# Output tiles in shared space, weight preparation four steps in, and paired column groups in an expert layer on one core

## The chip, the cores and the metric

One NeuronCore of a Trainium2 chip runs the whole program in one launch. The metric is the device time in microseconds (us); the program before took 934.85 us, the median of three runs (929.9 to 939.41).

## What is computed

Three stages follow each other. Stage one is a linear attention: `phi` projects queries and keys, takes exponentials, and num/den gives a token matrix x of 2304 x 512 floats. Stage two is a mixture of eight experts: each token goes to the expert with the largest gate logit, and

```
h = np.maximum(x[mask] @ w1[e], 0.0)            # 512 -> 1024
out[mask] = gate_w[mask, None] * (h @ w2[e])    # 1024 -> 512
```

Stage three is a gated network over all tokens:

```
a = x @ w_a;  b = x @ w_b                       # 512 -> 1536 each
return (a * b @ w_out).astype(np.float32)       # 1536 -> 512
```

The weights of stage three arrive as 64-bit floats; everything else is 32-bit, and the result is 32-bit. To keep 32-bit accuracy each operand of a matmul is split into a high and a low part (`mm3`, L51 to L54: three matmuls per product).

## The kernel before, in words

The kernel is written in a tile framework that places the semaphores and, for each engine, fixes one order of instructions at compile time by a planner: it walks the program in its own simulated time and gives a free engine the ready instruction with the smallest priority number. The number is the place in the program; `high_priority(offset=-LOWP)` adds 200 to it, so that such work yields to work written up to 200 instructions later. On the chip each engine then works through its fixed order, and an instruction that waits holds up all behind it. PE's order in stage three is written out by hand (`manual_schedule`).

**Stage two** (`Moe`, L518 on). The tokens of either half (two halves, `routes[0]` and `routes[1]`) are sorted by expert into tiles of 608 places, two groups of 304 columns each; here there are four tiles (called tile 0 to tile 3), with eight steps each, 32 steps in all (`run`, L603). In a tile's steps 0 to 3 `l1` runs for two f each (f = 0 to 7): for each column group 12 matmuls into a PSUM tile of one bank (`ps_l`, six buffers), then ScalarE writes `hh` (the rectified high part, L588) and VectorE `hl` (the rest, L589). In steps 4 to 7 `l2` runs: for each column group 24 matmuls over f = 0 to 7 (L600), then ScalarE copies the result (L601). Beside them: `loadw` and `splitw` bring the expert's weights (L542, L550, L551), and `gather` and `transp` bring the next tile's tokens in five pieces (L559, L571; their high and low parts `mxh` L574 and `mxl` L575); the transposes use the two buffers of `ps_t`, which the routing of the second half (`Route`, started from `side` at steps 0, 2, 4 and 6, L947) shares for its tables (`tbp`, `tbq`, L495).

**Weight preparation** (`Moe2.prep`, L699, with `narrow`, L677). The stage-three weights are cut into 12 pieces of f. `prep` turns one piece from 64 to 32 bits in two halves: a load `raw` of 768 KB (SyncE, L684), ScalarE (L688), GpSimd (L689), five VectorE instructions (L690 to L697); then sums (L706 to L709), the split into high and low (L714, L715), and four stores to `wsc` in DRAM (L716, L717). `raw` has two buffers in its pool. Eight pieces (NPRE) are prepared beside stage two, written at the steps `K0 + (K1 - K0) * f // 8`, which are steps 0, 3, 6, 10, 13, 16, 20 and 23 (L955 to L957). At step K1 = 27 `open_first` (L964) gives back their space and loads the first weights of stage three. The other four are prepared in stages 0, 2, 4 and 6 of stage three, from a second pool, `cv2` (L979 to L982).

**Between the two** stands a conditional (`tc.If`, L975) for more tiles than four; it is not entered here.

**Stage three** (`Moe2.run`, L779). There are 36 stages: three pairs of column blocks p, times 12 pieces f. A stage computes seven products `abp` (L830 to L834) in two PSUM buffers (`ps_l2`); ScalarE copies each out (`pc`, L836), VectorE combines them, and `outp` (L802) adds to six accumulators `op` (one bank each, one buffer each) for the stage before. After the last f of a p, `finish` (L784) scales the six accumulators into `o`, alternately on ScalarE (L793) and VectorE (L791), and GpSimd stores each by an indirect DMA (L794). `o` has OB = 2 buffers.

Of the kernel before, what the change touches and what calls it, by code (L numbers as in the profile page):

```python
# [10 lines left out]
F32 = mybir.dt.float32  # L11
F32R = mybir.dt.float32r
BF16 = mybir.dt.bfloat16
I32 = mybir.dt.int32
AF = mybir.ActivationFunctionType
ALU = mybir.AluOpType
AX = mybir.AxisListType
PSUM = bass.MemoryType.PSUM
ds = bass.ds

P = 128
# [3 lines left out]
DM = H * D  # L25
# [5 lines left out]
CG = 304  # L31
# [5 lines left out]
TB = 6  # L37
NPRE = 8
LOWP = 200
OB = 2  # L40
LOWP2 = 60
NWARM = 9
NATIVE = (0,)
# [3 lines left out]
def f32(ap):  # L47
    return ap.bitcast(F32)


def mm3(nc, out, lh, ll, rh, rl, start, stop):  # L51
    nc.tensor.matmul(out, lh, rh, start=start, stop=False)  # L52
    nc.tensor.matmul(out, lh, rl, start=False, stop=False)  # L53
    nc.tensor.matmul(out, ll, rh, start=False, stop=stop)  # L54
# [463 lines left out]
class Moe:  # L518
# [58 lines left out]
    def l1(self, T, f):  # L577
        nc = self.nc
        wh, wl = T["w", f // 2]
        for g in range(2):  # L580
            gs = slice(g * CG, g * CG + CG)
            ps = self.ps_l.tile([P, 512], F32, tag="l", name="hp")
            for c in range(4):
                i = 4 * (f % 2) + c
                mm3(nc, ps[:, :CG], wh[:, i, :], wl[:, i, :], T["xh"][:, c, gs], T["xl"][:, c, gs], c == 0, c == 3)
            hh = self.p_h.tile([P, CG], F32R, tag=f"h{f}{g}", name="hh")
            hl = self.p_h.tile([P, CG], F32R, tag=f"l{f}{g}", name="hl")
            nc.scalar.activation(hh, ps[:, :CG], AF.Relu)  # L588
            nc.vector.scalar_tensor_tensor(out=hl, in0=ps[:, :CG], scalar=0.0, in1=f32(hh), op0=ALU.max,  # L589
                                           op1=ALU.subtract)  # L590
            T["h", f, g] = (hh, hl)

    def l2(self, T, m):
        nc = self.nc
        wh, wl = T["w", 4 + m]
        for g in range(2):
            ps = self.ps_l.tile([P, 512], F32, tag="l", name="yp")
            for f in range(8):
                hh, hl = T["h", f, g]
                mm3(nc, ps[:, :CG], wh[:, f, :], wl[:, f, :], hh, hl, f == 0, f == 7)  # L600
            nc.scalar.copy(self.y[T["rt"].bp][:, m, ds(T["s"][g], CG)], ps[:, :CG])  # L601

    def run(self, tiles, side={}):  # L603
        NT, NJ = len(tiles), self.NJ
# [48 lines left out]
class Moe2:  # L653
# [13 lines left out]
    def pools(self, ctx, ps_a, ps_l):  # L667
        tc = self.tc
        pool = lambda n, b: ctx.enter_context(tc.tile_pool(name=n, bufs=b, side="right", reuse_waits="tile"))
        self.p_w[1] = pool("f_w1", 1)  # L670
        self.p_t[1] = pool("f_t1", 4)
        self.p_c = pool("f_c", 1)
        self.p_g = pool("f_g", 2)
        self.p_o = pool("f_o", OB)
        self.ps_a, self.ps_l = ps_a, ps_l

    def narrow(self, pool, f, half, dst, nt):  # L677
# [101 lines left out]
    def run(self, ws, ts, src0, side):  # L779
        nc, n = self.nc, self.N  # L780
        seq = [(p, f) for p in range(NTOK // n // 2) for f in range(self.NF)]
        accs, gs = {}, {}

        def finish(p):  # L784
            for m, acc in enumerate(accs.pop(p)):
                bp, b = divmod(2 * p + m // 3, HALF // n)
                o = self.p_o.tile([P, DM], F32, tag="o", name="o")
                c = b * (n // P) + m % 3
                g2 = self.routes[bp].g2[:, c:c + 1]
                if m % 2:  # L790
                    nc.vector.tensor_scalar(out=o, in0=acc, scalar1=g2, scalar2=None, op0=ALU.mult)  # L791
                else:
                    nc.scalar.activation(o, acc, AF.Copy, scale=g2)  # L793
                st = nc.gpsimd.indirect_dma_start(  # L794
                    out=self.out[:, :],
                    out_offset=bass.IndirectOffsetOnAxis(ap=self.routes[bp].perm[:, c:c + 1], axis=0),
                    in_=o[:, :], in_offset=None)
                for other in self.stores:
                    self.tc.declare_no_dep(st.ins, other, reason="each row of the output is stored once")
                self.stores.append(st.ins)  # L800

        def outp(k, m):  # L802
            p, f = seq[k]
            if f == 0 and m == 0:
                accs[p] = [self.ps_a.tile([P, 512], F32, tag=f"a{i}", name=f"op{i}") for i in range(6)]
            gh, gl = gs[k]
            wh, wl = ws[k](1536, 512)
            ms = slice(P * (m % 3), P * (m % 3) + P)
            mm3(nc, accs[p][m], gh[:, m // 3, ms], gl[:, m // 3, ms], wh, wl, f == 0, f == self.NF - 1)
            if m == 5:  # L810
                del gs[k], ws[k]
                if f == self.NF - 1:
                    finish(p)

        def stage(k):
            p, f = seq[k]
            ct = lambda tag, shape: self.p_c.tile([P] + shape, F32, tag=tag, name=tag)
            ca, u, d = ct("ca", [2, n]), ct("u", [2, n]), ct("d", [2, n])
            out = []
            gs[k] = [self.p_g.tile([P, 2, n], F32R, tag=t, name=t) for t in ("gh", "gl")]  # L820

            def gate(i, other):
                gh, gl = (x[:, i, :] for x in gs[k])
                nc.vector.tensor_mul(ca[:, i, :], ca[:, i, :], other)
                nc.scalar.copy(gh, ca[:, i, :])  # L825
                nc.vector.tensor_sub(gl, ca[:, i, :], f32(gh))  # L826

            for i, (col, t) in enumerate(self.PROD):
                ps = self.ps_l.tile([P, 512], F32, tag="l", name="abp")[:, :n]
                wh, wl = ws[k](col, 256)  # L830
                th, tl = ts[p][t]
                for c in range(2):
                    cs = slice(P * c, P * c + P)
                    mm3(nc, ps, wh[:, cs], wl[:, cs], th[:, c, :], tl[:, c, :], c == 0, c == 1)  # L834
                x = self.p_c.tile([P, n], F32, tag="pc", name="pc", bufs=5)
                nc.scalar.copy(x, ps)  # L836
                out.append(x)
                if i == 1:
                    nc.vector.tensor_add(u[:, 0, :], x, out[0])
                elif i == 2:  # L840
                    nc.vector.tensor_add(ca[:, 0, :], x, out[0])
                elif i == 3:
                    nc.vector.tensor_add(u[:, 1, :], x, u[:, 0, :])  # L843
                elif i == 4:
                    nc.vector.tensor_add(d, u, x.unsqueeze(1).to_broadcast([P, 2, n]))
                elif i == 5:
                    nc.vector.tensor_add(x, x, u[:, 1, :])
                    gate(0, x)
                elif i == 6:
                    nc.vector.tensor_add(ca[:, 1, :], x, d[:, 0, :])  # L850
                    gate(1, d[:, 1, :])
                if k and i > 1:
                    for m in (i - 2,) if i < 6 else (4, 5):
                        outp(k - 1, m)

        src = src0
        self.rest(src, ts[0])
        for k, (p, f) in enumerate(seq):
            with self.tc.high_priority(offset=-LOWP2):
                for st in side.get(k, ()):  # L860
                    st()
            if k + 1 < len(seq) and k + 1 not in ws:
                ws[k + 1] = self.weights(k + 1)
            if f == 0 and p:
                self.rest(src, ts[p])
            with self.tc.manual_schedule(engines={mybir.EngineType.PE}):
                stage(k)
            if f == self.NF - 2 and k + 2 < len(seq):
                src, ts[p + 1] = self.terms(p + 1, self.p_s)
        with self.tc.manual_schedule(engines={mybir.EngineType.PE}):  # L870
            for m in range(6):
                outp(len(seq) - 1, m)
# [13 lines left out]
def trn_kernel(ctx, tc, qk, v, w_phi, mod_id, w_gate, bias, wm, wf, out):  # L886
    nc = tc.nc
# [8 lines left out]
    tl = dict(reuse_waits="tile")  # L896
# [24 lines left out]
                       {5: rsteps[0:2], 6: rsteps[2:3], 7: rsteps[3:4]}.get(r, []) if r > 2 else [])  # L921
    with ExitStack() as mctx:
        ps_t = mctx.enter_context(tc.tile_pool(name="ps_t", bufs=2, space=PSUM, **tl))
        ps_l = mctx.enter_context(tc.tile_pool(name="ps_l", bufs=6, space=PSUM, **tl))
        ypool = ctx.enter_context(tc.tile_pool(name="y", bufs=1, **tl))
        y = [ypool.tile([P, 4, YC], F32, name=f"y{i}") for i in range(2)]
        m2 = Moe2(nc, tc, wf, wsc, y, routes, out, f64)
        mo = Moe(nc, tc, mctx, cst, xs, wm, y, ps_l, ps_t)
# [23 lines left out]
            with tc.high_priority(offset=-LOWP):  # L952
                m2.prep(f, cv[0], 2, 2)

        K0, K1 = 0, len(tiles) * mo.NJ - 5  # L955
        for f in range(NPRE):
            side.setdefault(K0 + (K1 - K0) * f // NPRE, []).append(lambda f=f: conv(f))  # L957
        ts, src0 = {}, []
# [24 lines left out]
    ps_a = ctx.enter_context(tc.tile_pool(name="ps_a2", bufs=1, space=PSUM, **tl))  # L983
    ps_l = ctx.enter_context(tc.tile_pool(name="ps_l2", bufs=2, space=PSUM, **tl))
    m2.pools(ctx, ps_a, ps_l)
    m2.run(ws, ts, src0[0], side)


# [55 lines left out]
```

## Time and profile before

| what | value |
|---|---|
| median of three runs | 934.85 us (929.9 to 939.41) |
| the profiled execution's own time | 940.45 us |
| its span, first to last instruction | 938.7 us |
| PE busy | 880.0 us (94%), granted clock 0.957 on the mean |
| VectorE (DVE) busy | 671.3 us (72%) |
| ScalarE (ACT) busy | 438.3 us (47%) |
| GpSimd (POOL) busy | 187.4 us (20%) |

The engines' busy time is a mean over the three stages. PE here is the matmul engine, PEld its weight loads, SP the SyncE queue that issues most DMAs. [...] Stage one ends at about 246 us, stage two at about 481 us, stage three's last matmul at 926.4 us.

### The profile page before, as it was taken

What the parts mean: (1) busy time and instruction counts of PE and PEld (TensorE: products, weight loads), DVE (VectorE), ACT (ScalarE), POOL (GpSimd) and SP (SyncE); (2) the same over time, 40 slices, a digit from 0 to 9 for tenths busy, and PEclk for the clock granted to TensorE, in tenths of its full rate; (3) what the DMA queues carried; (4) which work ended last, traced back from release to release, by engine and by line L of the source; (5) the groups of instructions that cost most, each with busy time, mean ns of one, the idle gap of its engine ahead of it and who ended that gap; (6) DMA issues with size and microseconds to landing.
All of it is one profiled execution on the core that took longest, in us unless ns stands there. A gap on an engine that the chain in (4) does not pass through costs nothing. (4 is left out here: it accounts for less than half of the span.)

```text
span 938.7 us, 15310 instructions
## 1 busy us (share of the span) xinstructions
PE 880.0 (94%) x5645; PEld 833.4 (89%) x5645; DVE 671.3 (72%) x1252; ACT 438.3 (47%) x806; POOL 187.4 (20%) x171
## 2 busy tenths in 40 slices
PE   6899999899799799999989999978999998999994
PEld 4899998899799799999988989967999998999993
DVE  7878899969799998986239889856454466554552
ACT  5577666555344454554324445444333344333332
POOL 6443333301343543220002111002000001000002
PEclk7999998899899799999989999979999999999998
DMA  7332330112567688795037998586666667766631
GB/s 246 102 104 77 105 105 13 29 57 64 199 203 268 245 287 307 277 322 188 29 131 290 371 317 312 189 305 206 213 202 205 203 201 244 223 203 202 202 124 67
DMA packets 74309, 179.21 MB, mean 191 GB/s; under 512 B 8912, under 2 KB 27808, under 8 KB 74224
## 3 DMA queue, kind: packets, MB, share of 16 engines
q1 hardware_dynamic: 71184, 168.39, 53.3%
q0 software_dynamic: 3040, 9.75, 3.1%
q8 instruction: 46, 0.75, 0.3%
q14 instruction: 39, 0.32, 0.1%
HBM read 140.36 MB, written 37.75 MB: 190 GB/s over the span
## 5 line engine op out<-in xcount | busy, mean ns | idle before, releaser
L836 ACT COPY pc<-abp 128x384 f32<-128x384 f32 x252 | 120.4, 479 | 195.6 <-PE abp L54 193.9
L52 PE MATMUL abp<-yh,fw 128*128 128x384 f32 x504 | 173.6, 344 | 16.1 <-DMA fw<-wsc 6.4
L54 PE MATMUL abp<-yh,fw 128*128 128x384 f32 x504 | 172.6, 342 | 0.2 <-DMA fw<-wsc 0.2
L53 PE MATMUL abp<-yl,fw 128*128 128x384 f32 x504 | 172.4, 342 | 0.0
L52 PEld LDWEIGHTS abp<-yh,fw 128*128 128x128 f32 x504 | 97.0, 192 | 25.9 <-ACT pc L836 7.6
L689 POOL TENSOR_SCALAR cvs<-cvs 128x768 f32<-128x768 f32 x24 | 59.2, 2468 | 250.4 <-ACT cvs L688 244.9
L53 PEld LDWEIGHTS abp<-yl,fw 128*128 128x128 f32 x504 | 97.0, 192 | 7.8
L54 PEld LDWEIGHTS abp<-yh,fw 128*128 128x128 f32 x504 | 96.7, 192 | 0.7 <-DMA fw<-wsc 0.7
L54 PE MATMUL op<-fw,gl 128*128 128x512 f32 x216 | 85.9, 398 | 1.3 <-DVE gl L826 1.3
L52 PE MATMUL op<-fw,gh 128*128 128x512 f32 x216 | 86.1, 398 | 1.0 <-ACT gh L825 1.0
L53 PE MATMUL op<-fw,gh 128*128 128x512 f32 x216 | 85.4, 395 | 0.0
L794 POOL DMA_INDIRECT out<-o,perm x18 | 17.7, 983 | 318.5 <-ACT o L793 311.7
L53 PE MATMUL hp<-mxl,wh 128*128 128x304 f32 x256 | 79.1, 310 | 1.5 <-DVE mxl L575 1.5
L52 PE MATMUL hp<-mxh,wh 128*128 128x304 f32 x256 | 79.5, 314 | 0.6 <-ACT mxh L574 0.6
L54 PE MATMUL hp<-mxh,wl 128*128 128x304 f32 x256 | 78.7, 308 | 0.0
L53 PE MATMUL yp<-hl,wh 128*128 128x304 f32 x256 | 77.3, 303 | 0.0
L52 PE MATMUL yp<-hh,wh 128*128 128x304 f32 x256 | 77.0, 303 | 0.0
L54 PE MATMUL yp<-hh,wl 128*128 128x304 f32 x256 | 77.0, 302 | 0.0
L236 PE MATMUL nmp<-kx,qts 128*128 128x73 f32 (+1 forms) x640 | 73.3, 271 | 1.8 <-DVE grest L478 1.8
L236 PEld LDWEIGHTS nmp<-kx,qts 128*128 128x128 f32 (+1 forms) x640 | 69.7, 187 | 4.0 <-issue 3.0
L185 ACT ACTIVATE qts<-qtp 128x512 f32<-128x512 f32 (+1 forms) x80 | 40.2, 552 | 47.0 <-PE qtp L182 46.8
L127 POOL TENSOR_TENSOR xtl<-qk,xth 128x512 fp32r<-128x512 f32 (+1 forms) x35 | 44.3, 1268 | 88.0 <-ACT xth L126 83.0
(201 smaller groups left out, 2052.9 us busy)
## 6 DMA issues: line engine op xcount, KB each, us to landing
fw<-wsc SPq DMA_DIRECT2D x72, 512.0 KB
fw<-wsc SPq DMA_DIRECT2D x144, 256.0 KB
raw<-in_moe_w SPq DMA_DIRECT2D x24, 768.0 KB
s<-in_moe_w SPq DMA_DIRECT2D x32, 512.0 KB
fw<-wsc SPq DMA_DIRECT2D x72, 128.0 KB
wsc<-whi SPq DMA_DIRECT2D x12, 640.0 KB
wsc<-wsum SPq DMA_DIRECT2D x12, 640.0 KB
wsc<-whi SPq DMA_DIRECT2D x12, 512.0 KB
```

The lines of the kernel that those rows point to most:

```text
L52: nc.tensor.matmul(out, lh, rh, start=start, stop=False)
L53: nc.tensor.matmul(out, lh, rl, start=False, stop=False)
L54: nc.tensor.matmul(out, ll, rh, start=False, stop=stop)
L127: (nc.vector if u == 0 else nc.gpsimd).tensor_sub(lo[:, x:y], src, f32(hi[:, x:y]))
L185: nc.scalar.activation(t[:, s, :n, :], ps[:, :n, :], AF.Exp, scale=1.0 - 2.0 * s)
L236: nc.tensor.matmul(ps[pp, o, :], qt[:, c, a, pp], st["kx", b][:, 2 * h + c, :], start=c == 0, stop=c == 1)
L689: nc.gpsimd.tensor_scalar(out=s.bitcast(F32), in0=s.bitcast(F32), scalar1=LEAST, scalar2=None, op0=ALU.max)
L794: st = nc.gpsimd.indirect_dma_start(out=self.out[:, :], out_offset=bass.IndirectOffsetOnAxis(ap=self.routes[bp].perm[:, c:c + 1], axis=0), ...
L836: nc.scalar.copy(x, ps)
```

## The change

Three edits stand in one diff.

In `finish` three accumulators now share one tile `os` of 3 x 512 floats, with tag `raw` in the pool `cv2`: it has the size of a `raw` tile (6144 bytes per partition) and takes its two buffers, so that six outputs have room at once. The pool `f_o` and OB are gone. The scaling and the stores are as before, each on a third of a tile.

K0 and K1 are 3 and 28: the eight preparations are written at steps 3, 6, 9, 12, 15, 18, 21 and 24, and `open_first` at step 28.

In `l1` one PSUM tile of two banks holds both column groups; after the 24 matmuls of an f there is one ScalarE and one VectorE instruction over 2 x 304 columns where there were two of each over 304. `hh` and `hl` are one tile per f. `l2` also takes a tile of two banks, a bank per group, and copies each bank as before. `ps_l` has three such tiles where it had six of one bank.

```diff
--- before.py
+++ after.py
@@ -37,7 +37,6 @@
 TB = 6
 NPRE = 8
 LOWP = 200
-OB = 2
 LOWP2 = 60
 NWARM = 9
 NATIVE = (0,)
@@ -577,28 +576,28 @@
     def l1(self, T, f):
         nc = self.nc
         wh, wl = T["w", f // 2]
+        ps = self.ps_l.tile([P, 2, 512], F32, tag="l", name="hp")
         for g in range(2):
             gs = slice(g * CG, g * CG + CG)
-            ps = self.ps_l.tile([P, 512], F32, tag="l", name="hp")
             for c in range(4):
                 i = 4 * (f % 2) + c
-                mm3(nc, ps[:, :CG], wh[:, i, :], wl[:, i, :], T["xh"][:, c, gs], T["xl"][:, c, gs], c == 0, c == 3)
-            hh = self.p_h.tile([P, CG], F32R, tag=f"h{f}{g}", name="hh")
-            hl = self.p_h.tile([P, CG], F32R, tag=f"l{f}{g}", name="hl")
-            nc.scalar.activation(hh, ps[:, :CG], AF.Relu)
-            nc.vector.scalar_tensor_tensor(out=hl, in0=ps[:, :CG], scalar=0.0, in1=f32(hh), op0=ALU.max,
-                                           op1=ALU.subtract)
-            T["h", f, g] = (hh, hl)
+                mm3(nc, ps[:, g, :CG], wh[:, i, :], wl[:, i, :], T["xh"][:, c, gs], T["xl"][:, c, gs], c == 0, c == 3)
+        hh = self.p_h.tile([P, 2, CG], F32R, tag=f"h{f}", name="hh")
+        hl = self.p_h.tile([P, 2, CG], F32R, tag=f"l{f}", name="hl")
+        nc.scalar.activation(hh, ps[:, :, :CG], AF.Relu)
+        nc.vector.scalar_tensor_tensor(out=hl, in0=ps[:, :, :CG], scalar=0.0, in1=f32(hh), op0=ALU.max,
+                                       op1=ALU.subtract)
+        T["h", f] = (hh, hl)
 
     def l2(self, T, m):
         nc = self.nc
         wh, wl = T["w", 4 + m]
+        ps = self.ps_l.tile([P, 2, 512], F32, tag="l", name="yp")
         for g in range(2):
-            ps = self.ps_l.tile([P, 512], F32, tag="l", name="yp")
             for f in range(8):
-                hh, hl = T["h", f, g]
-                mm3(nc, ps[:, :CG], wh[:, f, :], wl[:, f, :], hh, hl, f == 0, f == 7)
-            nc.scalar.copy(self.y[T["rt"].bp][:, m, ds(T["s"][g], CG)], ps[:, :CG])
+                hh, hl = T["h", f]
+                mm3(nc, ps[:, g, :CG], wh[:, f, :], wl[:, f, :], hh[:, g, :], hl[:, g, :], f == 0, f == 7)
+            nc.scalar.copy(self.y[T["rt"].bp][:, m, ds(T["s"][g], CG)], ps[:, g, :CG])
 
     def run(self, tiles, side={}):
         NT, NJ = len(tiles), self.NJ
@@ -671,7 +670,6 @@
         self.p_t[1] = pool("f_t1", 4)
         self.p_c = pool("f_c", 1)
         self.p_g = pool("f_g", 2)
-        self.p_o = pool("f_o", OB)
         self.ps_a, self.ps_l = ps_a, ps_l
 
     def narrow(self, pool, f, half, dst, nt):
@@ -784,7 +782,9 @@
         def finish(p):
             for m, acc in enumerate(accs.pop(p)):
                 bp, b = divmod(2 * p + m // 3, HALF // n)
-                o = self.p_o.tile([P, DM], F32, tag="o", name="o")
+                if m % 3 == 0:
+                    os = self.p_o.tile([P, 3, DM], F32, tag="raw", name="o", bufs=2)
+                o = os[:, m % 3, :]
                 c = b * (n // P) + m % 3
                 g2 = self.routes[bp].g2[:, c:c + 1]
                 if m % 2:
@@ -794,7 +794,7 @@
                 st = nc.gpsimd.indirect_dma_start(
                     out=self.out[:, :],
                     out_offset=bass.IndirectOffsetOnAxis(ap=self.routes[bp].perm[:, c:c + 1], axis=0),
-                    in_=o[:, :], in_offset=None)
+                    in_=o, in_offset=None)
                 for other in self.stores:
                     self.tc.declare_no_dep(st.ins, other, reason="each row of the output is stored once")
                 self.stores.append(st.ins)
@@ -921,7 +921,7 @@
                        {5: rsteps[0:2], 6: rsteps[2:3], 7: rsteps[3:4]}.get(r, []) if r > 2 else [])
     with ExitStack() as mctx:
         ps_t = mctx.enter_context(tc.tile_pool(name="ps_t", bufs=2, space=PSUM, **tl))
-        ps_l = mctx.enter_context(tc.tile_pool(name="ps_l", bufs=6, space=PSUM, **tl))
+        ps_l = mctx.enter_context(tc.tile_pool(name="ps_l", bufs=3, space=PSUM, **tl))
         ypool = ctx.enter_context(tc.tile_pool(name="y", bufs=1, **tl))
         y = [ypool.tile([P, 4, YC], F32, name=f"y{i}") for i in range(2)]
         m2 = Moe2(nc, tc, wf, wsc, y, routes, out, f64)
@@ -952,7 +952,7 @@
             with tc.high_priority(offset=-LOWP):
                 m2.prep(f, cv[0], 2, 2)
 
-        K0, K1 = 0, len(tiles) * mo.NJ - 5
+        K0, K1 = 3, len(tiles) * mo.NJ - 4
         for f in range(NPRE):
             side.setdefault(K0 + (K1 - K0) * f // NPRE, []).append(lambda f=f: conv(f))
         ts, src0 = {}, []
@@ -983,6 +983,7 @@
     ps_a = ctx.enter_context(tc.tile_pool(name="ps_a2", bufs=1, space=PSUM, **tl))
     ps_l = ctx.enter_context(tc.tile_pool(name="ps_l2", bufs=2, space=PSUM, **tl))
     m2.pools(ctx, ps_a, ps_l)
+    m2.p_o = cv[1]
     m2.run(ws, ts, src0[0], side)
```

## Rows read from the trace of the kernel before

**Rows 1.** Waits of PE, whole span: releaser, total us, times, longest us.
```profile
PE abp L52 <- DMA fw<-wsc: 6.4, 1, 6.4
PE abp L52 <- ACT pc L836: 6.1, 4, 2.9
...
PE abp L54 <- DMA fw<-wsc: 0.2, 1, 0.2
```

**Rows 2.** By stretch: us; PE, PEld, DVE, ACT, POOL busy (count); PEclk; DMA; GB/s.
```profile
246.00:313.50 67.50, 61.58 (x447) 60.63 (x445) 63.29 (x142) 31.38 (x51) 29.75 (x13) 0.93 0.61 205
...
373.60:427.30 53.70, 53.70 (x390) 53.69 (x391) 48.64 (x70) 27.28 (x45) 13.46 (x6) 1.00 0.85 302
427.30:484.70 57.40, 53.74 (x388) 53.49 (x386) 16.75 (x26) 17.76 (x34) 0.00 (x0) 0.99 0.21 67
...
926.50:938.70 12.20, 0.00 (x0) 0.00 (x0) 1.50 (x2) 1.37 (x2) 3.96 (x5) 0.65 0.29 109
```

**Rows 3.** Timeline around the middle finishes: start us, us, instruction [idle before <-releaser].
```profile
652.95 0.69 ACT L793 ACTIVATE o<-op,g 128x512 f32<-128x512 f32 x1 [2.23 <-DMA out<-o,perm]
...
654.06 0.69 PE L52 MATMUL abp<-yh,fw 128*128 128x384 f32 x1 [2.91 <-ACT pc L836]
...
797.34 0.69 PE L52 MATMUL abp<-yh,fw 128*128 128x384 f32 x1 [2.42 <-ACT pc L836]
```

**Rows 4.** Busy time and granted clock just after three stops of PE.
```profile
654.06:657.50 3.44, 3.44 (x10) 3.21 (x11) 2.22 (x4) 0.80 (x2) 1.78 (x2) 0.54 0.44 92
797.34:800.80 3.46, 3.46 (x10) 3.22 (x11) 2.22 (x4) 0.80 (x2) 1.78 (x2) 0.53 0.40 86
314.00:324.00 10.00, 10.00 (x56) 10.00 (x56) 8.00 (x20) 3.63 (x6) 3.24 (x2) 0.74 0.96 358
```

**Rows 5.** Timeline of GpSimd at the end: first, second and sixth store.
```profile
924.34 0.97 POOL L794 DMA_INDIRECT out<-o,perm  x1 [124.09 <-ACT o L793]
925.61 0.97 POOL L794 DMA_INDIRECT out<-o,perm  x1 [0.30 <-issue]
...
933.39 0.97 POOL L794 DMA_INDIRECT out<-o,perm  x1 [0.45 <-DVE o L791]
```

**Rows 6.** Timeline of PE between tile 0 and tile 1.
```profile
306.87 0.40 PE L495 MATMUL tbq<-tbqr,lhs 128*128 128x45 bf16 x9 [1.06 <-DVE top L942]
...
312.06 0.90 PE L571 MATMUL mxt<-ident,xg 96*128 96x96 f32 x4 [4.32 <-DVE mxl L575]
```

**Rows 7.** Timeline: second layer's first matmul and the last `hl`, tiles 0 to 2.
```profile
276.31 0.39 PE L52 MATMUL yp<-hh,wh 128*128 128x304 f32 x1
342.11 0.39 PE L52 MATMUL yp<-hh,wh 128*128 128x304 f32 x1
399.44 0.39 PE L52 MATMUL yp<-hh,wh 128*128 128x304 f32 x1
...
281.30 0.48 DVE L589 SCALAR_TENSOR_TENSOR hl<-hp,hh 128x304 fp32r<-128x304 f32 x1
347.99 0.46 DVE L589 SCALAR_TENSOR_TENSOR hl<-hp,hh 128x304 fp32r<-128x304 f32 x1
404.41 0.47 DVE L589 SCALAR_TENSOR_TENSOR hl<-hp,hh 128x304 fp32r<-128x304 f32 x1
```

**Rows 8.** VectorE out of PSUM, stage two: groups by shape, then one pair.
```profile
L589 DVE SCALAR_TENSOR_TENSOR hl<-hp,hh 128x304 fp32r<-128x304 f32 x64 | 29.3, 467 | 10.9 <-ACT hh L588 10.9
L575 DVE TENSOR_TENSOR mxl<-mxt,mxh 128x512 fp32r<-128x512 f32 x12 | 8.0, 678 | 0.0
L575 DVE TENSOR_TENSOR mxl<-mxt,mxh 128x384 fp32r<-128x384 f32 x4 | 2.2, 549 | 2.0 <-ACT mxh L574 2.0
...
431.36 0.85 DVE L589 SCALAR_TENSOR_TENSOR hl<-hp,hh 128x304 fp32r<-128x304 f32 x2
```

**Rows 9.** ScalarE's first instruction of a weight half: its group, and the longest wait.
```profile
L688 ACT ACTIVATE cvs<-raw 128x768 f32<-128x768 f32 x16 | 14.7, 917 | 31.6 <-DMA raw<-in_moe_w 29.7 <-DVE wsum L715 1.1 <-DVE wsum L697 0.8
...
360.05 0.90 ACT L688 ACTIVATE cvs<-raw 128x768 f32<-128x768 f32 x1 [6.79 <-DMA raw<-in_moe_w]
```

## The prediction, written before the changed kernel ran

> **What bounds the kernel now.** [...] The list of PE's waits comes first, since PE is busy in 94% of the span. Its longest entry is a wait for stage-three weights, 6.4 us, which the change does not touch; the next that a VectorE or ScalarE copy ends is `abp` behind `pc`, 6.1 us in four places [rows 1]. The busy time by stretch then shows which engine sets the pace: from tile 0 to its end VectorE is busy for 63.29 of 67.5 us, and in tile 2 for 48.64 of 53.7 beside a PE that never stops, while in tile 3 it needs 16.75 of 57.4 us [rows 2]. So in tiles 0 to 2 VectorE's fixed order is as full as PE's, and afterwards PE is alone. The timelines around the stops say what came last at each. [...]
>
> **Part one, room for six outputs.** It removes the waits of an output for the store of the one two before. At 652.95 ScalarE starts an `o` after 2.23 us of waiting for a store; the copies `pc` queue behind it, and PE, with two `abp` buffers, stops for 2.91 us. The same happens 143 us later, for 2.42 us [rows 3]. With six buffers ScalarE waits for the accumulator alone, which PE has long finished. That gives back 2.91 + 2.42 = 5.3 us, and the half clock behind them: (1 - 0.54) x 3.44 = 1.6 and (1 - 0.53) x 3.46 = 1.6 us [rows 4]. What is late next is nothing on PE: ScalarE has some 0.7 us per `o` more in a row, which two `abp` buffers covered at the first `o` of each finish. At the end no matmul runs any more [rows 2], and GpSimd's six stores set the end. The first two start at 924.34 and 925.61, 1.27 us apart with no wait between; the sixth starts at 933.39 [rows 5]. Without waits for buffers it starts at 924.34 + 5 x 1.27 = 930.7, so 2.7 us earlier, and the landing behind it moves along. The outputs are ready by then: the last accumulator is finished before 926.5, and its scaling takes 0.75 us on VectorE (1.50 us for two [rows 2]). Part one: 5.3 + 3.2 + 2.7 = 11.2 us. Below: nothing, if the thirds of a tile wait for each other; above: no row shows more to win. I take 11.2. A half tile is already treated by itself: the L54 matmul waited 0.2 us for the second DMA of a weight tile whose first had let L52 go [rows 1].
>
> **Part two, one pair in place of two groups.** It removes 32 ScalarE and 32 VectorE instructions in stage two and makes 32 of each longer. VectorE needs 678 - 549 = 129 ns for 128 more columns, about 1.01 ns each; one `hl` of 304 takes 467 ns, so one of 608 about 467 + 306 = 773 ns, against 0.85 us for two in a row [rows 8]. That is 0.08 us per pair. It counts in tiles 0 to 2, 24 pairs: 1.9 us, taken in full because VectorE is the full engine there; its lower end is 0, its upper 32 x 0.08 = 2.5. ScalarE's saving counts nothing, since it is busy for half of those stretches (31.38 of 67.5 us); were it full, the copies of `yp` would be late and PE would pay.
>
> [...]
>
> What the pair adds is a wait. The first group of f = 7 used to be emptied while the second was computed; now both come after the second. The second layer's first group needs f = 7 in its last three of 24 matmuls. A step of 48 matmuls takes 53.7 / 8 = 6.7 us at full clock [rows 2], so a group takes 3.35 and f = 7 comes 3.35 x 22 / 24 = 3.1 us after its start. Before, the last `hl` was needed one group later. The starts are 276.31, 342.11 and 399.44; the last `hl` ends at 281.78, 348.45 and 404.88 [rows 7]. With 0.3 us for the longer instruction PE would stand for 281.78 + 0.3 - 279.4 = 2.7, then 3.6 and 2.7 us, in sum 9.0, and three half clocks of 1.6 as in rows 4: 13.8 us at most. At least: nothing, if VectorE is earlier there. Behind the waiting matmul stand all of PE's queue, and nobody else waits for it soon.
>
> **Part three, the later preparation.** The work is the same; its place in the priorities is three steps later at the start and one at the end. Each piece moves two loads and four stores on SP, two instructions on POOL, four on ScalarE and 16 on VectorE past the steps' own work. What can be won is the stop between tile 0 and tile 1: PE waits 1.06 us for the routing table and 4.32 for `mxl` [rows 6], both VectorE's and both behind preparation in its order, and then runs ten microseconds at 0.74, which costs 2.6 [rows 4]: 8.0 us at most. What can be lost: a load that lands late ahead of ScalarE's copies, 6.79 us in the worst case, now hidden by six PSUM buffers [rows 9]. `open_first` one step later (6.7 us) costs nothing: tile 3 has 40.65 us of free VectorE time [rows 2], and the first stage-three weights are not used before that stretch ends at 484.7; without that cover PE would wait the 6.7.
>
> For the two open terms, up to 13.8 lost and up to 8.0 won, I take zero together. VectorE's order is full from tile 0 to tile 2, so a stop of PE at one point gives VectorE the time that the next stop would have taken; the nearest row is tile 2, full on both engines and without a stop.
>
> **Sum.** 940.45 us for the profiled execution, less 11.2 and 1.9: 927.35. That execution is 5.6 us above the median, and nothing in its rows says which term holds them, so the difference goes to the median: 934.85 - 13.1 = 921.75, say **922 us**.
>
> **The rivals.** (a) *Routing gets ahead.* The table's chain on VectorE no longer alternates with preparation, and the stop between the tiles goes without a new one: 922 - 8 = 914. For it: both waits there are for VectorE. Against: VectorE stays full, and preparation fills every gap that it finds, wherever it is written. Chance 0.20. (b) *The last pair is late.* The three waits of part two come in full: 922 + 13.8 = 936. For it: 5.4 to 6.3 us between the second layer's start and the last `hl` in all three tiles [rows 7]. Against: each stop lets VectorE catch up for the next. Chance 0.20. [...] (c) *The ring of three, slower than before.* A pair's buffer comes free after two other pairs, 6.7 us; six single banks gave five groups of 1.68, 8.4. ScalarE waits for `raw` loads 29.7 us in all in stage two [rows 9], and `hh` stands behind them. From a lag of 6.7 us on (tile 1's last `hl` is 6.3 us behind [rows 7]) PE pays each further microsecond; if it pays all of those waits, 922 + 29.7 = 952. Against: such waits fall in the second layer too, where PE has two tiles of 6.7 us in hand. Chance 0.06. (d) *Part one does not do what it says*: the thirds of one output tile wait for each other's stores, and 11.2 us stay: 933. Against it is the 0.2 us row above. Chance 0.06. The forecast, open terms within 6 us of zero, has 0.48.
>
> **Range and chances.** About 1% is what a measurement of this kernel can tell from no change: 925.5 and 944.2 are the bounds. The forecast's own range is 916 to 928, of which some 0.39 lies below 925.5; with (a) faster has 0.58. Same takes the rest of the forecast, (b) and (d): 0.35. Slower is (c) and a little beyond (b): 0.07. The range reaches to (a), down to 912, and to (b), up to 936.
>
> **What would show it.** Right: no ScalarE `o` that waits for a store; PE without stops of over 1 us near 654 and 797; the six last stores 1.27 us apart. For part two: `hl` at about 773 ns and 32 of them; the first stop of `yp` at `hl` would be (b). For part three: the wait for `mxl` between tiles 0 and 1 gone or not. Wrong would be a gain in stage two alone with the finishes as they are, or stops at `hp` for a PSUM buffer (c).

## The result: 1.1% faster, by part one alone

The changed kernel takes 927.15 us (median of 13 runs, 922.8 to 930.8), the kernel before 936.37 us (13 runs, 929.9 to 941.8). The ratio is 0.9892, with a 95% interval of 0.9871 to 0.9913. So about 9 to 10 us went (9.2 by the medians, 10.1 by the ratio), where 13.1 were forecast. Gains of whole runs below go by the ratios on record; a quotient of the medians differs from them by up to 2 us. The span of the profiled execution is 928.4 us, after 938.7.

I cut both executions at the same instructions of TensorE: the first `hp` (start of stage two), the first `abp` (start of stage three), the end of the last matmul. "After" is the changed kernel; e1, e2 and e4 are the experiments below.

| us | before | e4 (part three) | after | e1 (part one) | e2 (parts two, three) |
|---|---|---|---|---|---|
| to the first `hp` | 246.05 | 241.67 | 243.95 | 241.52 | 242.75 |
| stage two | 238.65 | 238.62 | 240.76 | 237.77 | 240.72 |
| stage three | 441.74 | 440.98 | 434.20 | 432.20 | 443.01 |
| last matmul to the end | 12.3 | 12.2 | 9.5 | 9.5 | 12.3 |

The part up to the first `hp`, which nothing here changes, differs by several microseconds between executions. The other lines repeat better: the end within 0.2 us, stage two within 1 us (237.8 to 238.7 in four executions with single groups in six banks, 239.8 to 240.8 in the three with pairs), stage three within some 2 us in this table. So stage three and the end became shorter with six outputs, stage two longer with the pairs.

The busy time by stretch of the changed kernel (us; PE, PEld, DVE, ACT, POOL busy with count; PEclk, the granted clock of PE as a share of full speed; DMA; GB/s): tile 0 to the start of tile 1's transpositions, tile 2, the former place of both finishes, and the end.

```profile
244.00:314.70 70.70, 65.34 (x471) 63.96 (x469) 66.41 (x141) 30.36 (x43) 32.75 (x13) 0.96 0.59 196
...
373.00:427.00 54.00, 52.67 (x382) 52.23 (x381) 44.97 (x58) 27.69 (x39) 12.21 (x6) 1.00 0.80 286
...
641.00:797.30 156.30, 156.05 (x810) 144.77 (x809) 88.00 (x149) 64.12 (x132) 12.29 (x12) 1.00 0.68 224
918.91:928.40 9.49, 0.00 (x0) 0.00 (x0) 0.75 (x1) 0.04 (x1) 4.02 (x5) 0.63 0.37 142
```

From 641 to 797 us PE is now busy for 156.05 of 156.30 us at a granted clock of 1.00: no stop near 654, none near 797, and so no half clock behind them [rows 3, 4]. ScalarE's three `o` of the first finish wait for their accumulator and not for a store (timeline of ScalarE, changed kernel: start, us, instruction, idle before and its releaser):

```profile
640.82 0.69 ACT L793 ACTIVATE o<-op,g 128x512 f32<-128x512 f32 x1 [0.51 <-PE op L53]
...
644.33 0.69 ACT L793 ACTIVATE o<-op,g 128x512 f32<-128x512 f32 x1 [0.17 <-PE op L53]
...
647.84 0.69 ACT L793 ACTIVATE o<-op,g 128x512 f32<-128x512 f32 x1 [0.22 <-PE op L53]
```

At the end the six stores stand one behind the other, 1.27 us apart, where the sixth came 9.05 us after the first [rows 5]. GpSimd's timeline, first, second and sixth store:

```profile
916.82 0.97 POOL L794 DMA_INDIRECT out<-o,perm  x1 [126.41 <-ACT o L793]
918.09 0.97 POOL L794 DMA_INDIRECT out<-o,perm  x1 [0.31 <-issue]
...
923.18 0.97 POOL L794 DMA_INDIRECT out<-o,perm  x1 [0.30 <-issue]
```

In stage two the stop between tile 0 and tile 1 is shorter, 3.13 where it was 4.32 us [rows 6], but small stops stand at new places (timeline of PE): `hp` and `yp` wait for the copies `y`, that is for a buffer, and once `yp` waits for an `hl`.

```profile
308.00 0.41 PE L51 MATMUL hp<-mxh,wh 128*128 128x304 f32 x1 [0.59 <-ACT y L600]
313.08 0.30 PE L570 MATMUL mxt<-ident,xg 96*128 96x96 f32 x1 [3.13 <-DVE mxl L574]
398.17 0.38 PE L51 MATMUL yp<-hh,wh 128*128 128x304 f32 x1 [1.33 <-DVE hl L588]
477.40 0.41 PE L51 MATMUL yp<-hh,wh 128*128 128x304 f32 x1 [0.73 <-ACT y L600]
```

The wait at 398.17 is one for a buffer too. The matmul is the first `yp` of tile 2 and reads `hh`; the `hl` that ends just before it is the sixth of the tile's eight, and with it a pair of banks comes free. The tile's last `hl` starts only at 402.51, and in no tile does a matmul wait for the last one, as rival (b) would have it (timeline of VectorE, the sixth and the eighth):

```profile
397.24 0.78 DVE L588 SCALAR_TENSOR_TENSOR hl<-hp,hh 128x608 fp32r<-128x608 f32 x1
...
402.51 0.78 DVE L588 SCALAR_TENSOR_TENSOR hl<-hp,hh 128x608 fp32r<-128x608 f32 x1
```

The merged copies are there, half as many and as long as worked out from [rows 8] (group by shape, stage two; busy us, mean ns):

```profile
L588 DVE SCALAR_TENSOR_TENSOR hl<-hp,hh 128x608 fp32r<-128x608 f32 x32 | 25.1, 784 | 5.1 <-ACT hh L587 5.1
```

### The profile page after: what moved, and what is told of

Same layout as the page of the kernel before. It is cut to its first block, busy times and chain, and to the rows that moved or that the text cites. A ratio compares the mean times of both kernels' runs of the same rounds, so it can differ in the third digit from the quotient of the medians.

```text
span 928.4 us, 15260 instructions
## 1 busy us (share of the span) xinstructions
PE 874.4 (94%) x5645; PEld 827.4 (89%) x5645; DVE 666.0 (72%) x1220; ACT 434.6 (47%) x774; POOL 188.2 (20%) x171
```

## The experiments

My theory after the result: part one is worth more than the whole gain, and the pairs cost some of it. The rivals: part of the gain comes from stage two's new order, or the preparation's place gives or takes something. First each part alone.

**e1, part one alone.** On the kernel before:

```diff
-                o = self.p_o.tile([P, DM], F32, tag="o", name="o")
+                if m % 3 == 0:
+                    os = self.p_o.tile([P, 3, DM], F32, tag="raw", name="o", bufs=2)
+                o = os[:, m % 3, :]
...
```

> Part one alone: six output buffers in the narrowing's space; stage two as before. Theory (room for outputs is the whole gain): stage three 7.5 us shorter (441.7 to about 434.2 us from the first abp to the last matmul), the tail behind the last matmul 12.2 to 9.5 us, no stop of PE near 654 or 797 us; in all 10.2 us off, a ratio of 0.989 to the kernel before. The prediction's own number for this part was 11.2 us, 0.988. Rival (the gain of the changed kernel came from stage two's new order, which brought the stages into another rhythm): under 6 us off, a ratio of 0.994 or more.

Measured: 923.26 us, a ratio of 0.9877 (0.9849 to 0.9906). That is 11.5 us (8.8 to 14.1), the whole gain and more. Against e4, whose order of instructions is that of the kernel before, stage three is 8.8 us shorter and the end 2.7. Of PE's waits for `pc` [rows 1] stage three has one left (total us, times, longest):

```profile
PE abp L51 <- ACT pc L836: 0.2, 1, 0.2
```

**e2, parts two and three without part one** (the changed kernel with the two outputs of before).

> Parts two and three together, outputs with two buffers as before. Theory: stage two 2.1 us longer as in the changed kernel, stops of 2.4 to 2.9 us near 654 and 797 us there as before, tail 12.2 us; in all 0 to +2 us, a ratio of 1.000 to 1.002. The prediction had 1.9 us off, 0.998. Rival (these two parts carry some of the gain): 4 us off or more, 0.996 or less.

Measured: 939.20 us, 1.0037 (1.0013 to 1.0061): slower, by less than a percent. The finishes stop PE as before, 2.86 and 3.20 us.

**e3, part two alone.**

> Part two alone: pairs in neighbouring banks, weight preparation from step 0 as before. Theory of the prediction: hl at 770 to 780 ns x32, 1.9 us off (0.998). Rival b (the last pair late): yp waits for hl in three tiles, up to 13.8 us more (1.015). Third reading, from the changed kernel: one short wait for hl, 0 to 2 us more (1.000 to 1.002).

Measured: 937.56 us, 1.0025 (1.0003 to 1.0047). The prediction's 1.9 us gain isn't there, nor are the 13.8 us of rival (b); the third reading holds.

**e4, part three alone.**

```diff
-        K0, K1 = 0, len(tiles) * mo.NJ - 5
+        K0, K1 = 3, len(tiles) * mo.NJ - 4
```

> Part three alone: preparation from step 3 to step 28 in place of 0 to 27, single groups as before. Theory of the prediction: the stop between tile 0 and 1 stays or moves, 0 within 2 us (0.998 to 1.002). Rival a (routing gets ahead): the stop for mxl goes, 8 us off (0.991). Rival d: a load of weights late ahead of ScalarE shows, up to 6.8 us more (1.007).

Measured: 935.31 us, 1.0005 (0.9977 to 1.0034). The stop for `mxl` stays at 4.32 us. Why nothing moves is seen in the fixed order of each engine's instructions, counted for the two programs (buffer numbers left out):

```
engine       SP   POOL    ACT    DVE     PE
before      815    294   1618   1703  11000
e4          815    294   1618   1703  11000
positions at which the two differ: 0 on each engine
```

Every engine gets the same sequence. It is the same too with preparation written in steps 8 to 28, and with all of it in step 27 at an offset of 2000 (built, not run). So in this kernel neither the place in the code nor the offset decides when preparation runs. What the planner goes by instead, these orders do not show. e2 and e3 have one order between them as well, so they measure the pairs twice: +0.37% and +0.25%, some 2.3 to 3.5 us.

Next, where the pairs lose. The waits of PE in stage two, of e1 (single groups) and then of e2 (pairs): releaser, total us, times, longest.

```profile
PE mxt L570 <- DVE mxl L574: 4.3, 1, 4.3
PE tbq L494 <- DVE top L942: 1.2, 1, 1.2
PE hp L51 <- ACT mxh L573: 0.6, 1, 0.6
PE hp L52 <- DVE mxl L574: 0.5, 1, 0.5
```

```profile
PE mxt L571 <- DVE mxl L575: 3.1, 1, 3.1
PE mxt L571 <- DMA xg<-xs,idx: 1.6, 1, 1.6
PE yp L52 <- DVE hl L589: 1.3, 1, 1.3
PE hp L52 <- ACT y L601: 1.2, 2, 0.6
PE yp L52 <- ACT y L601: 0.7, 1, 0.7
PE hp L52 <- ACT mxh L574: 0.7, 1, 0.7
```

The pairs win 2.9 us in three old waits (mxl 4.3 to 3.1, `top` 1.2 to 0, the second mxl 0.5 to 0) and lose 4.8 in new ones: 1.6 for a gather and 3.2 for buffers, 1.3 of them for one that an `hl` has yet to empty and 1.9 for those that `y` holds. Stage two as a whole is 1.2 us (e3) to 2.1 us (e2) longer than e4's; the rest of the 2.3 to 3.5 us is not placed.

**e5, the ring of three without the merge.** Pairs of banks, but a copy for each column group:

```diff
+        ps = self.ps_l.tile([P, 2, 512], F32, tag="l", name="hp")
...
+            nc.scalar.activation(hh[:, g, :], ps[:, g, :CG], AF.Relu)
+            nc.vector.scalar_tensor_tensor(out=hl[:, g, :], in0=ps[:, g, :CG], scalar=0.0, in1=f32(hh[:, g, :]),
+                                           op0=ALU.max, op1=ALU.subtract)
```

> The three two-bank buffers of part two alone: each column group still has its own ScalarE and VectorE copy (467 ns hl x64 as before), only the buffers are pairs; outputs and preparation as in the kernel before. Theory (the ring of three and the order of TensorE's work that comes with it cost the 2.3 us that the pairs alone lost): waits of hp for y as with the pairs, and nothing saved on VectorE: 2 to 5 us more, a ratio of 1.002 to 1.005. Rival (the merged copy, which empties one group later, is what costs): no wait for y or hl, 0 within 1.5 us (0.9985 to 1.0015).

Measured: 944.11 us, 1.0081 (1.0053 to 1.0109), more than expected. Its waits of PE in stage two:

```profile
PE hp L52 <- DVE hl L589: 6.3, 10, 1.3
...
PE yp L52 <- DVE hl L589: 3.6, 3, 1.8
PE hp L52 <- ACT y L601: 2.7, 2, 1.9
```

The old long stop for `mxl` is gone from the list, and ten short ones of `hp` for `hl` have come: PE finds no buffer free. So three two-bank buffers cost 7.6 us, and the merged copy gives 5.3 of them back (1.0081 to 1.0025). The rival, that the later emptying of the merge is what costs, falls. The planner orders PE's work differently in e3 and e5, so the two sizes hold for the buffers and the order that comes with them.

**e6, less VectorE.** On e1, one of the seven instructions of each weight half is left out in stage two, so that these weights get other values:

```diff
-        nc.vector.scalar_tensor_tensor(out=t, in0=hi, scalar=-0x40000000, in1=t,
-                                       op0=ALU.bitwise_and, op1=ALU.bitwise_or)
+        if f >= NPRE:
+            nc.vector.scalar_tensor_tensor(out=t, in0=hi, scalar=-0x40000000, in1=t,
+                                           op0=ALU.bitwise_and, op1=ALU.bitwise_or)
```

> Part one, and VectorE relieved in stage two: the 16 instructions of 0.95 us that merge sign and exponent in the first eight preparations are left out (the values of those weights are then others): 15.2 us off VectorE. Theory of the prediction (VectorE is the full engine of tiles 0 to 2, its time counts in full): about three quarters of it, 11 us, off the output alone, at most the 9 us that the stops in stage two and the clock behind them are worth: 914 to 917 us, a ratio to the kernel before of 0.977 to 0.980. Rival (VectorE's savings are swallowed, since TensorE waits for it at one point only): under 3 us beside the outputs alone, 0.9845 or more.

Measured: 923.01 us, 0.9847 (0.9812 to 0.9882), which the rival allows. In the profile stage two takes 232.51 us, 5.3 less than in e1, for 15.2 us of VectorE. Stage two of e1 and of e6 by busy time:

```profile
241.52:479.29 237.77, 227.34 (x1626) 225.88 (x1625) 181.09 (x319) 106.91 (x178) 64.40 (x30) 0.97 0.63 216
```

```profile
245.21:477.72 232.51, 224.86 (x1627) 223.91 (x1625) 167.06 (x303) 106.64 (x178) 63.75 (x30) 0.98 0.63 219
```

So by this one execution a microsecond less on VectorE is worth about 0.35 us of stage two, between the theory and the rival; the stop for `mxl` is still 2.9 us long. The whole program shows less: the median is 0.25 us below e1's, the ratio 0.3% with intervals that overlap, and stage three of the same execution takes 434.09 us, 1.9 more than in e1. A third is thus the upper reading, and a gain of the whole program over e1 is not shown.

**e7, an addition on GpSimd.** On e1:

```diff
-        nc.vector.tensor_add(dst, t.bitcast(F32), s.bitcast(F32))
+        (nc.gpsimd if f < NPRE else nc.vector).tensor_add(dst, t.bitcast(F32), s.bitcast(F32))
```

> Part one, and the last addition of each narrowing in the first eight preparations on GpSimd in place of VectorE: 16 x 0.94 = 15 us off VectorE, GpSimd, busy for 66 of 238 us in stage two, has some 35 us more. Theory (VectorE's time counts): 3 to 9 us off beside the outputs alone, a ratio to the kernel before of 0.978 to 0.985. Rival (swallowed, or the slower engine holds the buffers of the preparation longer): within 2 us of the outputs alone, 0.9855 to 0.990.

Measured: 937.40 us, 1.0010 (0.9983 to 1.0038): part one's gain is lost again, more than either side expected. Stage two takes 251.24 us, 13.5 more than in e1. PE waits 8.0 us for one gather, which GpSimd issues too, and VectorE isn't relieved (last section).

**e8, four outputs.** On e1, `if m % 2 == 0` for a new tile and `o = os[:, m % 2, :]`.

> Part one with two outputs in each of the two tiles, so four in flight in place of six. Theory (each output waits for the store of the one before it in its place): the middle finishes lose most of their stops, under 1 us each in place of 2.9 and 2.4; at the end the fifth store waits for the first two, 1 to 2.5 us later than with six; ratio to the kernel before 0.988 to 0.992. Rival (the place of the buffers, not their number, gives the gain): as with six, 0.9877 and a tail of 9.5 us.

Measured: 925.47 us, 0.9883 (0.9843 to 0.9923), the same as with six. There is no stop at the finishes, and the end is as short: third to sixth store on GpSimd,

```profile
911.83 0.97 POOL L794 DMA_INDIRECT out<-o,perm  x1 [0.30 <-issue]
913.10 0.97 POOL L794 DMA_INDIRECT out<-o,perm  x1 [0.31 <-issue]
914.37 0.97 POOL L794 DMA_INDIRECT out<-o,perm  x1 [0.30 <-ACT o L793]
915.65 0.97 POOL L794 DMA_INDIRECT out<-o,perm  x1 [0.30 <-issue]
```

The outputs do wait for stores, in four places, where with two outputs they did in eight and with six in none (all instructions that touch `o`, by what they waited for: us, times; the kernel before, then e8):

```profile
  DMA out<-o,perm: 21.7, 8
```

```profile
  DMA out<-o,perm: 7.0, 4
```

At the end that wait lies inside the 1.27 us that GpSimd takes for each store in front. My expectation of a later fifth store had left that out. By its end of 9.5 us e8 came out as the rival had it. That the waits shrink with the number, 21.7, 7.0 and none, speaks against the place of the buffers; two outputs in the new place, which would settle it, were not run.

**e9, four single banks.** The kernel before with `bufs=4` in place of 6 for the groups.

> Single groups as in the kernel before, with four PSUM banks for the groups in place of six; nothing else. Theory (what the pairs lose, they lose by how little work the buffers hold: three pairs let TensorE run at most two pairs, four groups, ahead of the copies): four single banks let it run three groups ahead, so stage two has waits of hp for hl and of yp for y that the kernel before lacks, 4 to 10 us more, a ratio of 1.004 to 1.011. Rival (the order of TensorE's work that comes with the pairs costs, not the buffers): with nearly the old order 0 to 1.5 us more, up to 1.0015.

Measured: 939.58 us, 1.0039 (1.0007 to 1.0071), at the theory's lower edge; the interval still holds the rival's 1.0015. PE's order differs from that of before at 526 of 11,000 positions (weight loads counted in; of the matmuls it is about a tenth), and these waits in stage two are new:

```profile
PE yp L52 <- DVE hl L589: 1.8, 2, 1.2
PE hp L52 <- DVE hl L589: 1.3, 3, 0.7
...
PE hp L52 <- ACT y L601: 1.1, 1, 1.1
```

Fewer buffers without a pair thus cost about what the pairs cost, by the middle values.

**e10, the layers apart.** The changed kernel with two two-bank buffers for `hp` and two single banks for `yp`:

```diff
-        ps = self.ps_l.tile([P, 2, 512], F32, tag="l", name="hp")
+        ps = self.ps_l.tile([P, 2, 512], F32, tag="l", name="hp", bufs=2)
...
+            ps = self.ps_l.tile([P, 512], F32, tag="y", name="yp", bufs=2)
```

> The changed kernel with its PSUM split by layer: two two-bank buffers for the pairs of the first layer, two single banks for the groups of the second, in place of three two-bank buffers for both. Theory (the shared ring of three makes hp wait for the copies y): those waits, 0.6 + 0.6 + 0.7 us, go; two pairs only let TensorE one pair ahead of the copies, which costs waits of hp for hl instead, 1 to 6 us; ratio to the kernel before 0.990 to 0.996. Rival (only the second layer's pairs cost): 2 us less than the changed kernel, 0.986 to 0.988.

Measured: 944.74 us, 1.0095 (1.0065 to 1.0125), far slower than either side said, though it has part one. Waits of PE in stage two:

```profile
PE yp L52 <- DVE hl L588: 8.6, 4, 4.2
PE hp L51 <- DVE hl L588: 6.8, 7, 2.0
```

The four waits of `yp` stand one in each tile, at a matmul that reads the last `hl`: 4.18, 2.69, 0.84 and 0.84 us. The first two (timeline of PE):

```profile
287.30 0.62 PE L52 MATMUL yp<-hl,wh 128*128 128x304 f32 x1 [4.18 <-DVE hl L588]
...
352.56 0.41 PE L52 MATMUL yp<-hl,wh 128*128 128x304 f32 x1 [2.69 <-DVE hl L588]
```

Here rival (b) is seen, 8.6 us in all where the prediction had worked out 9.0 before the clock, and beside it a pair's wait for a buffer (`hp` for `hl`), 6.8 us. In the changed kernel, though, the same later emptying keeps no matmul waiting for the last `hl`, so its cost hangs on the buffers and on the order that the planner finds with them; no run tells these two apart.

## Why the prediction was right, and where it was off

**Part one: right in place and size.** 11.2 us were worked out, e1 measured 11.5. Its terms: stops and half clock 8.5, measured 8.8 (e4 to e1); the end 2.7, measured 2.7. An agreement this close is in part luck, as stage three differs by some 2 us between executions of the same code (e1 and the changed kernel). Rival (d) falls: the thirds of an output tile don't wait for each other. In the changed kernel itself stage three wins only 7.5 us, since PE stops for 1.93 us at 557.08 us, where 0.49 stood before, and e1 doesn't stop. It is the same kind of wait at another store: a copy `whi` waits 3.17 us for the store of the last one, and `pc` queues behind it (timeline of ScalarE):

```profile
555.39 1.26 ACT L712 CAST whi<-wsum 128x1280 fp32r<-128x1280 f32 x1 [3.17 <-DMA wsc<-whi]
556.55 0.47 ACT L836 COPY pc<-abp 128x384 f32<-128x384 f32 x1
```

In e2 this wait is 2.00 us and PE's stop 0.78, so it differs between executions; the change doesn't touch that store.

**Part two: the failed step.** It was "taken in full because VectorE is the full engine there". The saving on VectorE is real: `hl` takes 784 ns where 773 were worked out, and stage two's busy VectorE falls from 182.35 us (e4) to 179.38 (e3). But by e6 at most about a third of such a saving reaches PE, so 1.9 would have been worth 0.7 or less. And a term that the sum left out, the coarser ring, was the larger one: 7.6 us for the ring (e5), 5.3 back for the merge, 2.3 to 3.5 us lost in all. Rival (c) named that ring and had a chance of 0.06. Its price was wrong, as it was hung on ScalarE's waits for `raw`; the rows of the changed kernel, e5 and e9 have PE waiting for `hl` and `y` at the first matmul of a group, that is for ordinary copies with too little room.

**Rival (b): a real wait, but not in the changed kernel.** 13.8 us were worked out from PE's old order. The planner chose another for the pairs: it runs the last three matmuls of the first group behind 11 and behind 21 of the next block's (matmuls in the second layer of tile 3, from the fixed order; m0 to m3 are the four output blocks):

```
before  m0 24, m0 24, m1 24, m1 24, m2 24, m2 24, m3 24, m3 24
after   m0 21, m1 11, m0 1, m1 10, m0 2, m1 3, m2 20, m0 24, m1 24, m2 4, m3 23, m2 24, m3 25
```

In tiles 0 to 2 the last two, which come with the last `hl`, stand behind 22 of the next block's; in tiles 0 and 1 the kernel before, too, runs 9 and 15 of the second group's ahead of the first group's last two. So `yp` is covered, and none of the three waits is left. But this order has three blocks open at once, each in a two-bank buffer, and that is where the waits for `y` (1.2 and 0.7 us) come from.

**Part three: it did nothing, for a reason that the prediction did not have.** Zero was taken from two open terms that were to cancel. Neither is there, so that zero came out is luck: no matmul waits for a last `hl`, and "two loads and four stores on SP, two instructions on POOL, four on ScalarE and 16 on VectorE past the steps' own work" are moved past nothing (e4). The kernel's description above gives the planner's rule by priority numbers; in this program it doesn't show. Rival (a) needed a move and so couldn't happen; the 3.13 in place of 4.32 us at the stop comes with the pairs (e3 has it too).

**The base.** The 5.6 us by which the profiled execution stood above the median were given to no term. Most of them lie ahead of stage two: e4, with the same order, reaches its first `hp` 4.4 us earlier and has the same stage two within 0.03 us.

The sum by measured terms: 11.5 less 2.3 to 3.5 is 8.0 to 9.2 us. By the same ratios the changed kernel gained 10.1 (8.1 to 12.1), so the terms add up within the noise. The total came out in the stated range because part one carries it; part two had the wrong sign. The faster version seems to be e1, part one alone: 0.9877, with the pairs left out. Its interval overlaps that of the changed kernel; that pairs cost something rests on e2 and e3, both above 1.

## What to carry to other kernels

A store that held an output buffer was paid here where the copies queued behind it, in stops of 2.91 and 2.42 us, and again in the clock, 0.54 and 0.53 over some 3.4 us behind each [rows 3, 4]; a few more buffers, in space that was free by then, gave both back (stage three 8.8 us shorter in e1), and four did as much as six (0.9883 and 0.9877). Before a move in the code is priced, compare the built order of the instructions: what a planner fills in at will may not move at all. And merging two copies out of PSUM had a gain and a price here, the instruction saved and the ring made coarser; count how many groups TensorE can run ahead before and after, since the coarser ring cost 7.6 us (e5) and the 32 saved instructions gave 5.3 back.

## What the hardware showed that I had not expected

An addition moved to GpSimd didn't relieve VectorE (e7): 16 additions of 962 ns left it, and its busy time in stage two rose from 181.09 to 185.42 us. Several of its other instructions became longer. Groups by shape in stage two (count, busy us, mean ns), in e1 and then in e7:

```profile
L690 DVE SCALAR_TENSOR_TENSOR cvt<-raw,cvt 128x768 int32<-128x768 int32 x16 | 15.4, 963 | 0.0
L695 DVE TENSOR_TENSOR wsum<-cvt,cvs 128x768 f32<-128x768 f32 x16 | 15.4, 962 | 0.6 <-DMA wsc<-wsum 0.6
...
L713 DVE TENSOR_TENSOR wsum<-wsum,whi 128x1024 fp32r<-128x1024 f32 x8 | 9.7, 1215 | 0.8 <-ACT whi L712 0.8
L688 DVE TENSOR_SCALAR cvt<-cvs 128x768 int32<-128x768 int32 x16 | 8.8, 553 | 1.8 <-POOL cvs L687 1.8
```

```profile
L690 DVE SCALAR_TENSOR_TENSOR cvt<-raw,cvt 128x768 int32<-128x768 int32 x16 | 18.6, 1163 | 0.1
...
L688 DVE TENSOR_SCALAR cvt<-cvs 128x768 int32<-128x768 int32 x16 | 13.7, 857 | 5.3 <-POOL cvs L687 5.3
L713 DVE TENSOR_TENSOR wsum<-wsum,whi 128x1024 fp32r<-128x1024 f32 x8 | 12.9, 1609 | 0.5 <-ACT whi L712 0.4
```

The copies `hl` out of PSUM kept their 465 ns (466), but so did the other `wsum` group of L713 its 1481 (1483), and L692 became shorter, 597 after 629. On GpSimd an addition takes 2440 ns, and GpSimd's busy time in stage two goes from 64.40 to 99.51 us. Whether that is what lengthens L690, L688 and one group of L713, and why `hl` and the other group of L713 would be spared, no row says. How much of e7's loss is this and how much the late gather, no run here separates.
